# Attention and mixer on one core: score couples of neighbouring pairs of heads, grouped two by two

## Chip, cores, metric

One core of a Trainium2 chip. The metric is the device time of one execution in microseconds (us). A kernel's quoted time is the median of its runs, and the runs of "before" beside it were made on the same chip. PE is the engine of the matmuls, DVE the vector engine, ACT the scalar engine, POOL the GpSimd engine; L363 is line 363 of the kernel.

## The reference

Cosine attention over 8 batches, 12 heads, 448 positions, 64 dimensions a head, followed by a mixer (a low-rank product along the sequence, then a two-layer perceptron with residual):

```python
q_n = q / (norm(q) + 1e-6);  k_n = k / (norm(k) + 1e-6)
scores = q_n @ k_n.T / tau
attn = softmax(scores)                    # exp(s - max) / (sum + 1e-9)
x = (attn @ v) laid out as [batch, seq, 768]
h = x.transpose(0, 2, 1) @ U @ V          # rank 32, along the sequence
u = x + h.transpose(0, 2, 1)
out = u + relu(u @ w_ch1) @ w_ch2         # 768 -> 3072 -> 768
```

## The kernel before

Two heads form a pair; there are 48 pairs, 6 a batch. For one pair, 64 + 64 dimensions lie on 128 partitions. Key chunks 0, 1 and 2 are scored by a *couple*: two matmuls of 64 contraction rows, one head on partitions 0 to 63 and one on 64 to 127, which run side by side (their starts lie 3 to 4 ns apart in the traces, and a couple behind a couple starts 0.196 us after it). The last 64 keys of both heads are packed into one matmul of 128 rows (chunk 3).

```python
def step_S(b, p, cs):                                   # scores and exponentials
    t = qkT[(b, p)];  e = E[(b * NP + p) % 2]
    for c in cs:
        sc = psum.tile([128, 2, 512], FP, name="sc", tag="ps_sc", bufs=2)
        if c == 3:                                      # full rows (L274)
            nc.tensor.matmul(out=sc[:, 0, 0:S], lhsT=t[:, 1, 384:512], rhs=t[:, 0, 0:S], ...)
            nc.scalar.activation(out=e[:, 6, 0:S], in_=sc[:, 0, 0:S], func=AF.Exp)
            continue
        for h in range(2):                              # a couple, half rows (L282)
            r = slice(64 * h, 64 * h + 64)
            nc.tensor.matmul(out=sc[:, h, 0:S], lhsT=t[r, 1, c * 128:(c + 1) * 128],
                             rhs=t[r, 0, 0:S], start=True, stop=True)
        nc.scalar.activation(out=e[:, 2 * c:2 * c + 2, 0:S], in_=sc[:, :, 0:S], func=AF.Exp)
```

The other steps of a pair, all with full-row matmuls: T (transposes of q and k, copied out by DVE as qkT), V in two halves V0 and V1 (probabilities by values, L302 and L309; DVE then makes X from the result), A (low-rank product with U, L331, and X moved into `up`, L342), H (product with V, L347). The mixer of the batch before (`mp`, L363 with w1 and L390 with w2) is cut into parts of six matmuls, which a list `fill` hands out between the steps by weights:

```python
for n in range(NPAIR + 1):
    ...
    parts = [now and S(0, 1), prev and V0, now and S(2, 3), prev and V1,
             nxt and T(n + 1), prev and A, prev and H]           # abridged
    weights = (2, 2, 2, 2, 2, 2, 1)
    for i, (fn, w) in enumerate(zip(parts, weights)):
        fn()
        # hooks for norms and loads at place i of pair n: after.pop((n, i)) ...
        # then as many mixer parts from `fill` as the weights give
```

In batch 0 (pairs 0 to 5) and at pair 6 there is no mixer work yet, so PE has nothing to fill its waits with.

Of the kernel before, what the change touches and what calls it, by code (L numbers as in the profile page):

```python
# [22 lines left out]
def kernel(  # L23
# [22 lines left out]
    NP = H // 2  # L46
# [207 lines left out]
    def step_T(b, p):  # L254
        gi, j = group_of[(b, p)]
        qn, kb, _ = norm[gi]
        tp = psum.tile([128, 8, 128], BF, name="tp", tag="ps_x", bufs=1)
        for i, t in ((0, qn), (1, kb)):
            for c in range(4):
                nc.tensor.transpose(out=tp[:, 4 * i + c, :], in_=t[:, j, c, :, :], identity=ident)  # L260
        t = work.tile([128, 2, 512], BF, name="qkT", tag="qkT", bufs=3)
        nc.vector.tensor_copy(out=t.rearrange("p a b -> p (a b)"),  # L262
                              in_=tp.rearrange("p a b -> p (a b)"))
        qkT[(b, p)] = t
        est.pe(0.46)
        est.dve(0.69)

    def step_S(b, p, cs):
        t = qkT[(b, p)]
        e = E[(b * NP + p) % 2]  # L270
        for c in cs:
            sc = psum.tile([128, 2, 512], FP, name="sc", tag="ps_sc", bufs=2)
            if c == 3:
                nc.tensor.matmul(out=sc[:, 0, 0:S], lhsT=t[:, 1, 384:512], rhs=t[:, 0, 0:S],  # L274
                                 start=True, stop=True)
                nc.scalar.activation(out=e[:, 6, 0:S], in_=sc[:, 0, 0:S], func=AF.Exp)
                est.pe(0.3)
                est.act(0.56)
                continue
            for h in range(2):  # L280
# [4 lines that stand above are left out]
            est.pe(0.25)  # L285
            est.act(0.93)
# [3 lines left out]
    def step_V(b, p, half):  # L290
        gi, j = group_of[(b, p)]
        vv = norm[gi][2]
        e = E[(b * NP + p) % 2]
        if half == 0:
            X_of[(b, p)] = work.tile([128, 4, 128], BF, name="X", tag="X", bufs=2)
        X = X_of[(b, p)]
        bank = psum.tile([128, 512], FP, name="av", tag="ps_av", bufs=1)
        av_of[(b, p)] = bank
        av = bank[:, 0:4 * (D + 1)].rearrange("p (i h d) -> p i h d", i=2, h=2)
        for i in range(2):  # L300
            ic = 2 * half + i
            nc.tensor.matmul(out=av[:, i, :, :], lhsT=e[:, 6, ic * 128:(ic + 1) * 128],  # L302
                             rhs=vv[:, 2 * j:2 * j + 2, 3, :],
                             start=(i == 0), stop=False, skip_group_check=True)
        for i in range(2):
            ic = 2 * half + i
            for h in range(2):
                for c in range(3):
                    nc.tensor.matmul(out=av[:, i, h, :],  # L309
                                     lhsT=e[:, 2 * c + h, ic * 128:(ic + 1) * 128],  # L310
                                     rhs=vv[:, 2 * j + h, c, :],
                                     start=False, stop=(i == 1 and h == 1 and c == 2),
                                     skip_group_check=True)
        rd = work.tile([128, 4, 1], FP, name="rd", tag="rd", bufs=4)
        nc.vector.reciprocal(out=rd, in_=av.rearrange("p i h d -> p (i h) d")[:, :, D:D + 1])  # L315
        nc.vector.tensor_mul(  # L316
            X[:, 2 * half:2 * half + 2, :].rearrange("p i (h d) -> p i h d", h=2),
            av[:, :, :, 0:D],
            rd.rearrange("p (i h) o -> p i h o", h=2).to_broadcast([128, 2, 2, D]))
        est.pe(0.52)  # L320
        est.dve(0.6)


    def u_of(b):
        return uE if b % 2 == 0 else uO

    def step_A(b, p):
        X = X_of[(b, p)]
        ap = av_of[(b, p)][:, 384:512]
        for c in range(4):  # L330
            nc.tensor.matmul(out=ap, lhsT=U_sb[:, c, :], rhs=X[:, c, :],  # L331
                             start=False, stop=(c == 3), skip_group_check=True)
        A = work.tile([128, 128], BF, name="A_sb", tag="A_sb", bufs=2)
        nc.scalar.copy(out=A, in_=ap)  # L334
        A_of[(b, p)] = A
        est.pe(0.44)
        est.act(0.3)
        up = psum.tile([128, S], FP, name="up", tag="ps_x", bufs=1)
        up_of[(b, p)] = up
        for c in range(4):  # L340
            n = 128 if c < 3 else 64
            nc.tensor.matmul(out=up[:, c * 128:c * 128 + n], lhsT=X[:, c, :], rhs=ident[:, 0:n],  # L342
                             start=(c == 0), stop=False, skip_group_check=True)

    def step_H(b, p):
        up = up_of[(b, p)]
        nc.tensor.matmul(out=up, lhsT=A_of[(b, p)], rhs=V_sb,  # L347
                         start=False, stop=True, skip_group_check=True)
        nc.vector.tensor_copy(out=u_of(b)[:, p, 0:S], in_=up)  # L349
        est.pe(0.19)  # L350
        est.dve(0.62)
        if b % 2 == 1 and p == NP - 1:
            nc.vector.tensor_copy(out=uO[:, :, S:512], in_=uE[:, :, 384:S])


    def steps_m1(b):
        u = u_of(b)
        o = 64 if b % 2 == 0 else 0

        def one(f):  # L360
            mp = psum.tile([128, S], FP, name="mp", tag="ps_m", bufs=2)
            for cc in range(CC):
                nc.tensor.matmul(out=mp, lhsT=w1_sb[:, cc, f * 128:(f + 1) * 128],  # L363
                                 rhs=u[:, cc, 0:S], start=(cc == 0), stop=(cc == CC - 1))
            est.pe(1.13)
            if est.act_first(0.55, 0.62):
                nc.scalar.activation(out=relu[:, f, o:o + S], in_=mp, func=AF.Relu)  # L367
            else:
                nc.vector.tensor_scalar_max(out=relu[:, f, o:o + S], in0=mp, scalar1=0.0)  # L369

        return [lambda f=f: one(f) for f in range(NC)]
# [59 lines left out]
    pairs = [(b, p) for b in range(B) for p in range(NP)]  # L431
# [50 lines left out]
    for gi in range(1, len(groups)):  # L482
        m, n, g = first_pair[gi], groups[gi][2], preps[gi]
# [23 lines left out]
    for n in range(NPAIR + 1):  # L507
        b, p = pairs[n] if n < NPAIR else (B, 0)
        prev = pairs[n - 1] if n > 0 else None
        now, nxt = n < NPAIR, n + 1 < NPAIR  # L510
        parts = [
            now and (lambda: step_S(b, p, (0, 1))),
            prev and (lambda: step_V(*prev, 0)),
            now and (lambda: step_S(b, p, (2, 3))),
            prev and (lambda: step_V(*prev, 1)),
            nxt and (lambda: step_T(*pairs[n + 1])),
            prev and (lambda: step_A(*prev)),
            prev and (lambda: step_H(*prev)),
        ]
        weights = [w if part else 0 for part, w in zip(parts, (2, 2, 2, 2, 2, 2, 1))]  # L520
        left = NP - p + 0.85 if p else 0.85
        nf = len(fill) if p == 0 else int(round(len(fill) / left))
        given = acc = 0
        for fn in after.pop((n, -1), []):
            fn()
        for i, (fn, w) in enumerate(zip(parts, weights)):
            if fn:
                fn()
            for g in after.pop((n, i), []):
                g()  # L530
            acc += w
            want = nf * acc // sum(weights)
            for _ in range(min(want - given, len(fill))):
                fill.pop(0)()
            given = want
        if p == 0 and n > 0:
            while fill:
                fill.pop(0)()
            fill.extend(steps_m1(b - 1) + steps_m2(b - 1))
# [38 lines left out]
```

## Time and profile before

| | before |
|---|---|
| median of 6 runs (3 of them made beside the changed kernel) | 648.82 us (648.52 to 649.09) |
| span of the profiled run | 646.9 us |
| PE busy | 94% of the span |
| DVE, ACT busy | 42%, 42% |
| mean granted clock of PE | 0.995 |

### The profile page before, as it was taken

Reading aid. Unit: us, or ns where it says so; the run is one execution under the profiler, and the core shown is the slowest. Engines: PE = TensorE matmul, PEld = TensorE weight load, DVE = VectorE, ACT = ScalarE, POOL = GpSimd, SP = SyncE. Lnnn points to the kernel's source line nnn. Section 1 sums busy time; section 2 is a strip of 40 time slices with the busy share of each in tenths; the row PEclk is TensorE's granted clock in tenths of the full one; section 3 lists DMA queues with packets and bytes.
Section 4 is the critical chain, followed back from the end, with each engine's and each line's share of the span. In section 5 each row is a group of like instructions: output and inputs, shape, how many; then the busy total and the mean of one; then the engine's idle time right before and its main releaser. Section 6 shows DMA issues by size and latency. Waiting matters only on the chain.

```text
span 646.9 us, 12173 instructions
## 1 busy us (share of the span) xinstructions
PE 609.4 (94%) x5160; PEld 360.4 (56%) x5160; DVE 273.3 (42%) x524; ACT 273.3 (42%) x501; POOL 195.2 (30%) x158
## 2 busy tenths in 40 slices
PE   1467999999999999999999999999999999999997
PEld 0244556655566556665566655665566555665564
DVE  4788335355244455364353453463442543210000
ACT  2465554345433454345433455334523454324310
POOL 7877244043141341340431431431404401000000
PEclk9997999999999999999999999999999999999999
DMA  7899991350315420161315302044311100001011
GB/s 195 196 220 234 233 241 43 98 147 4 83 35 126 110 73 16 32 168 48 86 26 135 95 24 79 25 117 105 87 25 26 50 1 1 25 25 26 1 50 49
DMA packets 51782, 54.33 MB, mean 84 GB/s; under 512 B 5552, under 2 KB 48112, under 8 KB 51728
## 3 DMA queue, kind: packets, MB, share of 16 engines
q1 hardware_dynamic: 44288, 43.14, 26.1%
q0 software_dynamic: 7120, 10.18, 8.6%
q8 instruction: 40, 0.66, 0.4%
q10 hardware_dynamic: 320, 0.23, 0.1%
q14 instruction: 14, 0.11, 0.1%
HBM read 52.02 MB, written 11.01 MB: 97 GB/s over the span
## 4 chain that ended last, share of the span: by engine, by line
PE 91%; DVE 6%; DMA 1%; ACT 0%; issue 0%; SPq 0%; ACTq 0%
PE mp L390 34%; PE mp L363 34%; PE av L309 5%; PE sc L282 5%; PE tp L260 3%; PE sc L274 2%; DVE qn L241 2%; PE av L302 2%; PE av L331 2%; DVE ss L215 1%; PE up L342 1%; PE mp L399 1%; PE up L347 1%; DVE qkT L262 1%; DVE X L316 1%; DMA kst<-in_k_dram 1%
## 5 line engine op out<-in xcount | busy, mean ns | idle before, releaser
L390 PE MATMUL mp<-w_sb,relu 128*128 128x384 bf16 x1344 | 246.8, 326 | 0.0
L390 PEld LDWEIGHTS <-relu 128*128 128x128 bf16 x1344 | 123.7, 98 | 77.9 <-issue 7.4
L241 POOL TENSOR_TENSOR kb<-kst,inv 128x512 bf16<-128x512 f32 x46 | 59.3, 1310 | 336.3 <-DVE inv L233 284.8
L363 PEld LDWEIGHTS <-w_sb 128*128 128x128 bf16 x1152 | 106.0, 98 | 92.9 <-issue 7.8
L284 ACT ACTIVATE E<-sc 128x896 bf16<-128x896 f32 x144 | 126.3, 917 | 46.3 <-PE sc L282 46.2
L367 ACT ACTIVATE relu<-mp 128x448 bf16<-128x448 f32 x156 | 84.7, 543 | 134.4 <-PE mp L363 134.4
L363 PE MATMUL mp<-uE,w_sb 128*128 128x448 bf16 x576 | 122.9, 353 | 1.1 <-DVE uE L349 1.1
L363 PE MATMUL mp<-uO,w_sb 128*128 128x448 bf16 x576 | 118.0, 353 | 0.0
L404 ACT COPY o_sb<-mp 128x384 f32<-128x384 f32 x50 | 23.9, 478 | 109.0 <-PE mp L399 109.0
L215 DVE TENSOR_REDUCE ss<-sq 128x16 f32<-128x1024 f32 (+1 forms) x50 | 58.1, 1166 | 3.3 <-ACT sq L207 3.3
L315 DVE RECIPROCAL rd<-av 128x4 f32<-128x4 f32 x96 | 17.1, 178 | 95.4 <-PE av L309 95.4
L241 DVE TENSOR_TENSOR qn<-qst,inv 128x512 bf16<-128x512 f32 x48 | 53.4, 1150 | 0.0
L282 PE MATMUL sc<-qkT 64*128 64x448 bf16 x288 | 45.5, 368 | 8.2 <-DVE qkT L262 6.1
L210 POOL TENSOR_TENSOR sq<-kst 128x1024 f32<-128x1024 f32 x23 | 52.0, 2262 | 2.7 <-DMA qst<-in_q_dram 2.7
L309 PE MATMUL av<-v,E 128*128 128x65 bf16 x1152 | 52.8, 195 | 0.0
L369 DVE TENSOR_SCALAR relu<-mp 128x448 bf16<-128x448 f32 x36 | 22.5, 625 | 67.0 <-PE mp L363 67.0
L262 DVE COPY qkT<-tp 128x1024 bf16<-128x1024 bf16 x48 | 33.0, 687 | 36.7 <-PE tp L260 36.7
L309 PEld LDWEIGHTS <-E 128*128 128x128 bf16 x1152 | 46.2, 98 | 0.0
L210 POOL TENSOR_TENSOR sq<-qst 128x1024 f32<-128x1024 f32 x23 | 43.5, 1892 | 0.0
L316 DVE TENSOR_TENSOR X<-av,rd 128x256 bf16<-128x256 f32 x96 | 40.8, 425 | 3.3
L334 ACT CAST A_sb<-av 128x128 bf16<-128x128 f32 x48 | 12.6, 263 | 61.7 <-PE av L331 61.7
L349 DVE CAST uO<-up 128x448 bf16<-128x448 f32 x24 | 14.9, 623 | 53.9 <-PE up L347 53.9
(66 smaller groups left out, 394.7 us busy)
## 6 DMA issues: line engine op xcount, KB each, us to landing
out_dram<-o_sb SPq DMA_DIRECT2D x54, 192.0 KB, 2.7
w_sb<-in_moe_w_ch_dram POOLq DMA_DIRECT2D x8, 1152.0 KB, 27.0
qst<-in_q_dram SPq DMA_DIRECT2D x23, 256.0 KB, 3.9
vst<-in_v_dram SPq DMA_DIRECT2D x46, 128.0 KB, 2.9
kst<-in_k_dram SPq DMA_DIRECT2D x44, 128.0 KB, 3.7
qst<-in_q_dram SPq DMA_DIRECT2D x23, 192.0 KB, 4.0
vst<-in_v_dram SPq DMA_DIRECT2D x46, 96.0 KB, 2.8
kst<-in_k_dram SPq DMA_DIRECT2D x44, 96.0 KB, 3.4
```

What stands on the lines that cost most here:

```text
L210: nc.gpsimd.tensor_mul(sq[:, 0:self.nh * 4, :], self.flat(t), self.flat(t))
L215: nc.vector.reduce_sum(self.ss[:, j, 0:self.nh * 4], self.sq[j][:, 0:self.nh * 4, :], axis=AX.X)
L241: eng.tensor_mul(o[:, j, :, :, :], t[:, 2 * j:2 * j + 2, :, :].rearrange("p h c d -> p c h d"), iv.unsqueeze(3).to_broadcast([128, 4, 2, D]))
L262: nc.vector.tensor_copy(out=t.rearrange("p a b -> p (a b)"), in_=tp.rearrange("p a b -> p (a b)"))
L282: nc.tensor.matmul(out=sc[:, h, 0:S], lhsT=t[r, 1, c * 128:(c + 1) * 128], rhs=t[r, 0, 0:S], start=True, stop=True)
L284: nc.scalar.activation(out=e[:, 2 * c:2 * c + 2, 0:S], in_=sc[:, :, 0:S], func=AF.Exp)
L309: nc.tensor.matmul(out=av[:, i, h, :], lhsT=e[:, 2 * c + h, ic * 128:(ic + 1) * 128], rhs=vv[:, 2 * j + h, c, :], start=False, stop=(i == ...
L316: nc.vector.tensor_mul(X[:, 2 * half:2 * half + 2, :].rearrange("p i (h d) -> p i h d", h=2), av[:, :, :, 0:D], rd.rearrange("p (i h) o -> ...
L363: nc.tensor.matmul(out=mp, lhsT=w1_sb[:, cc, f * 128:(f + 1) * 128], rhs=u[:, cc, 0:S], start=(cc == 0), stop=(cc == CC - 1))
L367: nc.scalar.activation(out=relu[:, f, o:o + S], in_=mp, func=AF.Relu)
L390: nc.tensor.matmul(out=mp, lhsT=relu[:, f, r0:r0 + 128], rhs=w2_sb[:, f, half * HC:(half + 1) * HC], start=(f == 0), stop=False, skip_grou ...
L404: nc.scalar.copy(out=o[:, cols], in_=mp)
```

## The change

The intent: run score couples of two neighbouring pairs back to back, so that PE changes between half rows and full rows less often. From pair 6 on, two pairs have three groups of two couples, in place of two groups of two and two single couples.

```diff
-        parts = [
-            now and (lambda: step_S(b, p, (0, 1))),
...
-        weights = [w if part else 0 for part, w in zip(parts, (2, 2, 2, 2, 2, 2, 1))]
+        if n < NP:
+            order = [ ... as before ... ]
+        elif n % 2 == 0:
+            order = [
+                (0, 2, now and (lambda: step_S(b, p, (0, 1)))),
+                (1, 2, lambda: step_V(*prev, 0)),
+                (2, 2, now and (lambda: step_S(b, p, (3,)))),
+                (4, 2, nxt and (lambda: step_T(*pairs[n + 1]))),
+                (3, 2, lambda: step_V(*prev, 1)),
+                (5, 1, lambda: step_A(*prev)),
+                (-2, 1, nxt and (lambda: (step_S(b, p, (2,)), step_S(*pairs[n + 1], (0,))))),
+                (6, 1, lambda: step_H(*prev)),
+            ]
+        else:
+            order = [
+                (0, 2, lambda: step_S(b, p, (1, 2))),
+                (1, 2, lambda: step_V(*prev, 0)),
+                (2, 2, lambda: step_S(b, p, (3,))),
+                ... V1, T, A, H as before ...
+            ]
+        parts = [fn for _, _, fn in order]
+        weights = [w if fn else 0 for _, w, fn in order]
```

Note that in even pairs the transposes T also move ahead of V1, and that V1 comes closer to A.

More of the change, by code (lines that the diff above doesn't have):

```diff
@@ L510 @@
         now, nxt = n < NPAIR, n + 1 < NPAIR
-        parts = [
-            now and (lambda: step_S(b, p, (0, 1))),
-            prev and (lambda: step_V(*prev, 0)),
-            now and (lambda: step_S(b, p, (2, 3))),
-            prev and (lambda: step_V(*prev, 1)),
-            nxt and (lambda: step_T(*pairs[n + 1])),
-            prev and (lambda: step_A(*prev)),
-            prev and (lambda: step_H(*prev)),
-        ]
-        weights = [w if part else 0 for part, w in zip(parts, (2, 2, 2, 2, 2, 2, 1))]
+        if n < NP:
+            order = [
+                (0, 2, now and (lambda: step_S(b, p, (0, 1)))),
+                (1, 2, prev and (lambda: step_V(*prev, 0))),
+                (2, 2, now and (lambda: step_S(b, p, (2, 3)))),
+                (3, 2, prev and (lambda: step_V(*prev, 1))),
+                (4, 2, nxt and (lambda: step_T(*pairs[n + 1]))),
+                (5, 2, prev and (lambda: step_A(*prev))),
+                (6, 1, prev and (lambda: step_H(*prev))),
+            ]
+        elif n % 2 == 0:
+            order = [
+                (0, 2, now and (lambda: step_S(b, p, (0, 1)))),
+                (1, 2, lambda: step_V(*prev, 0)),
+                (2, 2, now and (lambda: step_S(b, p, (3,)))),
+                (4, 2, nxt and (lambda: step_T(*pairs[n + 1]))),
+                (3, 2, lambda: step_V(*prev, 1)),
[4 more added lines that the diff above has]
+        else:
+            order = [
+                (0, 2, lambda: step_S(b, p, (1, 2))),
+                (1, 2, lambda: step_V(*prev, 0)),
+                (2, 2, lambda: step_S(b, p, (3,))),
+                (3, 2, lambda: step_V(*prev, 1)),
+                (4, 2, nxt and (lambda: step_T(*pairs[n + 1]))),
+                (5, 2, lambda: step_A(*prev)),
+                (6, 1, lambda: step_H(*prev)),
+            ]
+        parts = [fn for _, _, fn in order]
+        weights = [w if fn else 0 for _, w, fn in order]
         left = NP - p + 0.85 if p else 0.85
```

## The prediction

> **What bounds the kernel now.** I read the page first, then the PE's list of waits, then the chain of work in order of time around a score step. The page's busy lines, its slice line of PE and its chain line:
>
> ```profile
> PE 609.4 (94%) x5160; PEld 360.4 (56%) x5160; DVE 273.3 (42%) x524; ACT 273.3 (42%) x501; POOL 195.2 (30%) x158
> ...
> PE   1467999999999999999999999999999999999997
> ...
> PE 91%; DVE 6%; DMA 1%; ACT 0%; issue 0%; SPq 0%; ACTq 0%
> ```
>
> PE is full from the fifth slice of 16 us on, and the end is set by PE. The list of PE's waits names 32.9 us in all; the same list asked for 66 us onwards is empty. So after batch 0 there is no wait to take away: only PE's own time counts, and it is read from spacings of matmuls, because neighbours overlap in their recorded durations (353 ns recorded against a spacing of 0.19 us below). Two stretches of the chain, a lone score couple followed by the full-row score matmul, and two couples back to back (columns: start us, us, what):
>
> ```profile
> 301.96 0.38 PE mp L363 x2
> 302.34 0.29 PE sc L282 x2
> 302.63 0.30 PE sc L274
> 302.93 1.14 PE mp L363 x6
> ```
> ```profile
> 311.29 1.13 PE mp L363 x6
> 312.42 0.49 PE sc L282 x4
> 312.91 1.24 PE mp L363 x6
> ```
>
> A mixer matmul of 448 columns takes its turn every 0.189 us (1.13/6). A couple, two 64-row matmuls side by side, should cost one such turn, since its two matmuls start 3 to 4 ns apart. It costs 0.29, and the full-row matmul that follows costs 0.30, not 0.19. With two couples together the four cost 0.49 = 2 x 0.19 + 0.11, and the six full-row matmuls after them 1.24 instead of 1.13. So each passage from full rows to half rows costs about 0.10 us, each passage back about 0.11, and the step from couple to couple nothing.
>
> [...] in the first listing 0.29 + 0.30 - 2 x 0.189 = 0.21 us for in and out, in the second 0.49 + 1.24 - 2 x 0.189 - 1.13 = 0.22. [...]
>
> **The change, part by part.** Arithmetic and operands stay; from pair 6 on the order differs, and the order of both programs shows the same 5160 matmuls.
>
> [...] A pair has three couples (0, 1, 2) and one full-row score matmul (3). Before, each pair runs {0,1} and later {2} then 3: two groups. After, an even pair runs {0,1}, then 3 alone, and near its end {2 with 0 of the next pair}; the odd pair runs {1,2}, then 3. Three groups in two pairs instead of four. Counting runs of couples in the built order gives 95 before and 74 after, 21 fewer: even pairs 6 to 46. Each is worth one passage in and out: 21 x 0.214 = 4.5 us. That is on the path wherever PE never waits, so the whole of it from pair 8 on.
>
> Moved, first: the exponentials. At 20 of the 21 sites (pair 6 apart), between the joined group {2,0'} and {1',2'} lie two mixer parts and the matmul with V. From couple 0' to couple 1' that is 0.28 (way out) + the parts + 0.10 (way in): with two w2 parts 12 x 0.163 + 0.189 + 0.37 = 2.5 us, with two w1 parts 12 x 0.189 + 0.189 + 0.37 = 2.8. Couple 2' comes 0.20 later, and it needs the buffer that the exponential of 0' frees. In this trace the exponential starts 0.40 to 0.54 us after its couple (0.54 where a relu is before it in ACT's queue), a second in a row starts 0.81 later (the two in a row of pair 27 take 1.72 together), so that of 0' ends 0.4 to 0.54 - 0.2 + 0.81 + 0.92 = 1.9 to 2.1 us after couple 0'. In batch 0 a waiting matmul starts about 0.05 us after such an end (exponential ending at 39.49, matmul at 39.54). Needed at 2.7, there at 2.1: slack 0.6. No wait.
>
> Moved, second: step V1 now comes after the transposes and just one or two mixer parts ahead of the low-rank step A, which needs V1's result from DVE. In the trace V1's last matmul is followed by the reciprocal after 0.23 us (0.28 beside w1 parts) and the product X is complete 0.87 us (0.91) after that matmul starts; A starts 0.055 after X. That makes 0.93 (0.97). Distance now: at six sites one w2 part, 0.03 + 0.98 = 1.01; at three sites one w1 part, 1.17; elsewhere two parts, 2 or more. Before, the shortest was 2.4 (but for the last two pairs). So 0.08 us of slack at six sites, if DVE is free when V1 ends. What stands before V1 in DVE's queue is the copy of the transposes, 0.69, and the inversion of norms, 0.18 + 0.35, together 1.2 from 0.2 after the transposes; V1 ends 1.5 after them. Free by 0.1 to 0.25. Charge: 0 us, with up to 0.3 at each if I am wrong.
>
> Moved, third: the seam at pair 6, where there are no mixer parts to fill in. Here I walk all queues with the durations of this trace. The lines of DVE there now:
>
> ```profile
> 58.32 1.21 DVE L215 TENSOR_REDUCE ss<-sq 128x16 f32<-128x1024 f32 x1
> 59.56 0.18 DVE L218 TENSOR_SCALAR ss<-ss 128x32 f32<-128x32 f32 x1
> ...
> 60.52 0.35 DVE L233 RECIPROCAL inv<-ss 128x32 f32<-128x32 f32 x1
> 60.79 0.63 DVE L262 COPY qkT<-tp 128x1024 bf16<-128x1024 bf16 x1
> 61.33 2.69 DVE L241 TENSOR_TENSOR qn<-qst,inv 128x512 bf16<-128x512 f32 x2
> ```
>
> After: the copy of the transposes goes at 59.66, the inversion 60.3 to 60.87, V1's reciprocal only then, X done at 61.42, A at 61.47 (60.34 now), its second half straight after instead of at 61.47, the joined group at 61.97, V's product at 62.45. Then couples 1' and 2' directly: they wait for exponentials that end near 63.3 and 64.1, and mixer work begins at 64.44 (62.43 now). But now its sixth matmul waits 1.06 us for DVE's copy of u and goes at 64.61; after, that copy is done in time and the sixth goes at 65.4. Net 0.79 later with one couple more done (0.19): a loss of 0.6 us, once.
>
> Added: nothing. ACT and DVE get the same work; a few evacuations change engine (103 rows of relu and output copies on ACT in the built order before, 112 after, where repeats share a row), and neither engine bounds.
>
> Sum: -4.5 + 0.6 = -3.9. 648.8 - 3.9 = 644.9 us, 0.6% less.
>
> **The rivals.** (1) [...] grouped couples use both score buffers at once, so {1',2'} could stand on PE for 0'. For it: that is what happens in batch 0, and pair 6 will. Against: 0.6 us of slack with filler in between, and PE's empty list of waits after 66 us. If my slack were all wrong by a microsecond, 20 sites x 0.4 = 8 us, and the time would be 653. (2) A waits for X: nine tight sites. Against: DVE is 42% busy and each slack came out positive. For: 0.08 us is thin. At 0.3 us each 2.7 us are lost, 647.6. (3) [...] the full-row matmul 3, now alone, might keep its 0.30. Against: that 0.30 is the way back from half rows, seen in front of mixer matmuls as well. If it did, nothing is gained: 649.4. (4) Pair 6 goes better than walked: 644.3.
>
> **Range and chances.** The saving is arithmetic on spacings that repeat to a few ns, so the range comes from the seam (0 to 1.2) and from thin slacks (0 to 2): 643.8 to 646.6. Faster by over 2% would need 13 us, three times all that 21 passages hold: 0.01. Slower by over 2% needs a stall of 0.8 us at every site: 0.02. Within 2%: 0.97.
>
> **What would show it.** In the profile after: four half-row matmuls in every group from pair 6 on; 0.49 for each and 0.19 for a lone full-row score; a list of waits from 66 us on that is still empty, or has only hundredths for A on X. The seam: PE waits near 62.5 to 64.2 for exponentials, and the wait for u gone. The span up to the first mixer work longer, all later stretches shorter by 0.2 us in every two pairs. Wrong, if PE shows many waits of score matmuls on ACT after 66 us, or if lone couples and joined ones prove equally dear.

The sum is -4.5 + 0.6 = -3.9 us, estimated from spacings and durations in the trace of the kernel before. The prediction reads PE from starts and spacings, and walks the other engines in the program's order, which was the assumption; at the seam it put A at 61.47 us, 61.9 with the 0.4 by which the run came later to it, and A came at 62.0.

## More of the kernel before

PE's granted clock is the share of full speed at which it was allowed to run.

The page's row of PE's granted clock, in tenths per slice of 16 us, is short; it will matter:

```profile
PEclk9997999999999999999999999999999999999999
```

A digit below 9 in the fourth slice says that PE ran with less than its full clock for part of the time from 48 to 65 us.

## The result, and the profile after

The changed kernel took 646.32 us, the median of 6 runs (645.90 to 647.66). The ratio to the kernel before is 0.9964, with a 95% interval of 0.9951 to 0.9977. Ratios here are the mean time of one kernel's fast runs over that of the other's in the same rounds, so not quite the ratio of the medians. The gain is 2.5 us by the medians, against 3.9 predicted; it is clear of noise, and well within the 2% that the prediction gave.

The chain of work of the changed kernel in order of time (start us, us, what) has a lone full-row score matmul, and a joined group with the next group two mixer parts behind it:

```profile
302.57 1.14 PE mp L363 x6
303.71 0.19 PE sc L274
303.89 2.27 PE mp L363 x12
```
```profile
310.93 0.48 PE sc L282 x4
311.42 1.24 PE mp L363 x6
312.66 0.19 PE up L347
312.85 1.14 PE mp L363 x6
313.98 0.48 PE sc L282 x4
314.47 1.24 PE mp L363 x6
```

The full-row score matmul now costs its bare turn of 0.19, and the mixer after it costs 2.27 for 12, nothing extra. Each group costs 0.48 and leaves 0.10 in the matmuls after it (1.24 in place of 1.14). The group that comes close behind starts without a wait.

To see where the time went I cut both traces at the first 65-column V matmul of chosen pairs (us, from the matmuls' starts; "seam" is the stretch in which the new order begins):

| stretch | before | after | difference |
|---|---|---|---|
| start to the first transpose | 13.06 | 13.30 | +0.24 |
| first transpose to V0 of pair 5 (batch 0) | 43.77 | 43.93 | +0.16 |
| V0 of pair 5 to that of pair 7 (seam) | 20.39 | 23.30 | **+2.91** |
| pair 7 to pair 45 (38 pairs) | 474.93 | 470.86 | **-4.07** |
| pair 45 to pair 47 | 21.69 | 21.47 | -0.22 |
| pair 47 to the end | 73.01 | 73.02 | +0.01 |

The steady part gained exactly what was predicted: 4.07 us over 38 pairs is 0.214 for every two. The seam gave most of it back in this run. (The traced run of the changed kernel was the slowest of its six, 647.66 us, so that the rows add up to -1.0 us, and not to the 2.5 of the medians.) The list of PE's waits of the changed kernel (us in total, times, longest) has one new large entry, the 2.3:

```profile
PE av L331 <- DVE X L316: 4.4, 4, 2.3
```

The timeline of PE at the seam of the changed kernel shows where it lies (start us, us; in brackets the idle time before and its releaser):

```profile
59.20 0.54 PE L309 MATMUL av<-v,E 128*128 128x65 bf16 x12
62.03 0.38 PE L331 MATMUL av<-X,U_sb 128*128 128x128 bf16 x4 [2.29 <-DVE X L316]
62.25 0.36 PE L342 MATMUL up<-ident,X 128*128 128x128 bf16 x4
62.54 0.66 PE L282 MATMUL sc<-qkT 64*128 64x448 bf16 x4
63.13 0.55 PE L347 MATMUL up<-V_sb,A_sb 128*128 128x448 bf16 x1
63.92 0.56 PE L282 MATMUL sc<-qkT 64*128 64x448 bf16 x2 [0.23 <-ACT E L284]
64.72 0.56 PE L282 MATMUL sc<-qkT 64*128 64x448 bf16 x2 [0.25 <-ACT E L284]
65.21 2.42 PE L363 MATMUL mp<-uE,w_sb 128*128 128x448 bf16 x6
```

The 2.29 us wait of A and the two short waits of couples for ACT were in the walk. What was not is the last line: six mixer matmuls take 2.42 us of recorded time here, where 1.30 is usual. The window view gives the clock (columns: stretch, us, busy time and count of PE, its weight loads, DVE, ACT, POOL, then the granted clock):

```profile
56.10:62.80 6.70, 3.87 (x58) 2.61 (x57) 5.95 (x12) 2.90 (x7) 3.30 (x4) 1.00 1.15 235
62.90:69.60 6.70, 6.22 (x33) 2.76 (x30) 2.87 (x5) 3.89 (x5) 6.32 (x4) 0.50 1.15 233
```

In the 6.7 us after the wait PE had half its clock, just as the mixer work began. In the kernel before, the only half-clock window on record (the traces have the clock from about 30 us on) lay from 49.6 to 56.5, in batch 0, and the same stretch ran at full clock:

```profile
63.00:70.00 7.00, 5.94 (x57) 3.37 (x56) 2.77 (x6) 3.91 (x8) 5.60 (x4) 1.00 1.15 230
```

The clock row of the page has, accordingly, a second dent (the 8 in the fifth slice):

```profile
PEclk9997899999999999999999999999999999999999
```

### The profile page after: what moved, and what is told of

Its sections match the earlier page's. It is cut to its first block, busy times and chain, and to the rows that moved or that the text cites. A ratio compares the mean times of both kernels' runs of the same rounds, so it can differ in the third digit from the quotient of the medians.

```text
span 645.9 us, 12169 instructions
## 1 busy us (share of the span) xinstructions
PE 608.9 (94%) x5160; PEld 364.2 (56%) x5160; DVE 267.2 (41%) x512; ACT 282.3 (44%) x513; POOL 194.7 (30%) x158
## 4 chain that ended last, share of the span: by engine, by line
PE 92%; DVE 5%; DMA 1%; ACT 1%; SPq 0%; issue 0%
PE mp L363 34%; PE mp L390 34%; PE av L309 5%; PE sc L282 5%; PE tp L260 3%; PE av L302 2%; PE av L331 2%; PE up L342 2%; DVE ss L215 1%; PE mp L399 1%; PE up L347 1%; PE sc L274 1%; DVE qn L241 1%; DVE qkT L262 1%; DMA qst<-in_q_dram 1%; DVE X L316 1%
## 5 line engine op out<-in xcount | busy, mean ns | idle before, releaser
L367 ACT ACTIVATE relu<-mp 128x448 bf16<-128x448 f32 x162 | 88.2, 544 | 132.9 <-PE mp L363 132.9
L284 ACT ACTIVATE E<-sc 128x896 bf16<-128x896 f32 x144 | 124.1, 917 | 20.4 <-PE sc L282 20.0
L363 PE MATMUL mp<-uE,w_sb 128*128 128x448 bf16 x576 | 124.6, 356 | 0.0
L404 ACT COPY o_sb<-mp 128x384 f32<-128x384 f32 x56 | 26.7, 477 | 99.7 <-PE mp L399 99.7
L282 PE MATMUL sc<-qkT 64*128 64x448 bf16 x288 | 42.6, 370 | 8.5 <-DVE qkT L262 6.1
L369 DVE TENSOR_SCALAR relu<-mp 128x448 bf16<-128x448 f32 x30 | 18.7, 625 | 41.4 <-PE mp L363 41.4
```

Source lines behind the costliest of these rows:

```text
L363: nc.tensor.matmul(out=mp, lhsT=w1_sb[:, cc, f * 128:(f + 1) * 128], rhs=u[:, cc, 0:S], start=(cc == 0), stop=(cc == CC - 1))
L367: nc.scalar.activation(out=relu[:, f, o:o + S], in_=mp, func=AF.Relu)
L404: nc.scalar.copy(out=o[:, cols], in_=mp)
```

## The experiments

All gave correct results except the two "narrow" ones, which are wrong.

### 1. The changed kernel again

No edit.

> The changed kernel once more, as it is. My theory: in the steady part it gains 0.21 us per two pairs as predicted, and at the seam at pair 6 it loses more than I predicted, because step A waits 2.3 us there and PE's granted clock then falls to half for one or two windows of 3.4 us. As these windows do not fall alike in every run, this kernel's times should spread by over 1 us (645.9 to 647.7 before), low where the mean granted clock is 0.994 and high where it is 0.989, and the median should be near 646.3. Rival: the spread is noise of the chip; then the kernel before should spread as much in the same rounds, and the time should not go with the clock.

Measured: 647.23 us (646.43 to 647.71, 5 runs), ratio 0.9974 (0.9962 to 0.9987), before 648.61 (648.31 to 649.28) in 9 runs. The profiled run again had a half-clock window from 62.4 to 69.3, and by the same cuts as above its seam was 23.30 and pair 7 to 45 was 470.86, both as in the first trace of this kernel to the hundredth. (Such windows are 6.8 us long in both traces of this kernel, and 3.4 in those of experiments 2 and 3.) The spread was 1.3 us, against 1.0 in the kernel before. The expectation that time goes with the mean clock failed: of two runs with a mean clock of 0.995 one took 647.10 and one 647.43, as slow as those with 0.989. The kernel before spread nearly as much in the same rounds, which is what the rival, noise of the chip, expected. The mean says how long the half clock lasted, not on which work it fell, and only one run in each set has a trace that shows that; so what spreads the times stays open.

### 2. The new order from pair 8

```diff
-        if n < NP:
+        if n < NP + 2:
```

> The new order starts at pair 8 in place of pair 6; pairs 6 and 7 keep the old order. It saves 20 passages in place of 21. My theory (the seam costs what is missing): 648.8 - 20 x 0.214 = 644.5 us, spread like that of the kernel before (0.3 us), one half-clock window only, wait of A on X in pair 6 back at 0.7 us. Rival (the seam is harmless, each passage is worth less than 0.21 us or something in the steady part loses it): 646.3 + 0.1, no better than the changed kernel.

Measured: 644.85 us (644.03 to 645.37), ratio 0.9938 (0.9925 to 0.9950). It beats the changed kernel by 2.4 us on the same chip, with one passage less saved. Pair 7 to 45 is again 470.86. Its seam took 20.97, and even that has a half-clock window of 3.4 us in it (62.1 to 65.6), a second one; so "one window only" was not met in this run, and the spread of 1.3 us was larger than expected. The rival, that the seam is harmless, is out.

### 3. The reordering alone, without joined groups

```diff
-                (0, 2, lambda: step_S(b, p, (1, 2))),        # odd pairs
-                (2, 2, lambda: step_S(b, p, (3,))),
+                (0, 2, lambda: step_S(b, p, (0, 1))),
+                (2, 2, lambda: step_S(b, p, (2, 3))),
# even pairs: (3,) becomes (2, 3); the joined group is taken out; T stays ahead of V1
```

> The old grouping of couples ({0,1}, then {2} with 3) in all pairs, but in even pairs from 6 on the transposes come before V1 as in the changed kernel. My theory: moving V1 gains nothing in the steady part and loses at the seam, where A waits some 2 us for X: 649 to 651 us, steady stretches equal to those of the kernel before within 0.1 us per two pairs. Rival (the reordering itself gives the gain, not the joined groups): about 646.

Measured: 649.10 us (648.95 to 650.76), ratio 1.0006 (0.9993 to 1.0020). Pair 7 to 45 took 474.93, the figure of the kernel before to the hundredth: moving T and V1 gives and costs nothing in the steady part. Its seam took 21.48, 1.1 more than before, with a wait of A on X of 1.9. So the gain is from the joined groups alone, and a loss at the seam comes with the reordering (this trace, too, had a half-clock window there, from 63.4 to 66.8).

### 4. PE kept busy through the wait at the seam

```diff
-                (3, 2, lambda: step_V(*prev, 1)),
+                (3, 2, lambda: (step_V(*prev, 1), keep_busy(10) if n == NP else None)),
# keep_busy: 10 matmuls of 448 columns with ident and U_sb into a free mp buffer, never read
```

> The changed kernel with 10 useless matmuls of 448 columns (1.9 us of PE work) after V1 of pair 6, where PE waits 2.3 us for X anyway; their result is never read. My theory (the wait lets the granted clock fall to half, and that is what the seam costs beyond the 0.6 us): no half-clock window near 63 us, mean clock 0.994 to 0.995, and 644.9 us, the figure that the prediction gave, 1.4 less than the changed kernel, with small spread. Rival (the lost time is the wait of A itself and of the couples behind it): no faster than the changed kernel, 646.3 or more.

Measured: 645.04 us (644.11 to 645.77), ratio 0.9942 (0.9930 to 0.9955), 2.2 less than the changed kernel in the same rounds although 10 matmuls were added. The timeline of PE at its seam:

```profile
57.99 0.54 PE L309 MATMUL av<-v,E 128*128 128x65 bf16 x12
58.37 2.05 PE L511 MATMUL mp<-U_sb,ident 128*128 128x448 bf16 x10
60.82 0.38 PE L331 MATMUL av<-X,U_sb 128*128 128x128 bf16 x4 [0.40 <-DVE X L316]
...
63.81 1.31 PE L363 MATMUL mp<-uE,w_sb 128*128 128x448 bf16 x6
```

A starts 2.83 us after the V1 matmuls here (60.82 - 57.99), and 2.83 in the changed kernel (62.03 - 59.20): the added work neither hurried nor held up A, which waits for DVE. But the six mixer matmuls take 1.31, not 2.42, and the clock is full:

```profile
63.00:70.00 7.00, 6.56 (x66) 4.00 (x64) 2.17 (x6) 4.41 (x8) 5.01 (x3) 1.00 1.15 231
```

By the cuts, the seam took 20.97 in place of 23.30. So 2.3 us of the seam's loss were the half clock, and 0.6 remain (20.97 - 20.39). The old order's seam itself measures 20.36 to 20.61 in the traces of experiments 6 to 8, so these tenths are uncertain by some 0.2: against the first trace of experiment 7 (20.61), which like this one has no half clock in batch 0 or the seam, 0.4 remain. With the passage that is saved there added, that is 0.6 to 0.8, where the prediction had 0.6. Only one of the five runs has a trace; that the others were mostly spared too is read from their median. In this traced run there was no half-clock window on record before the end, so batch 0 was 0.7 shorter too; the same happened by chance in other runs (experiment 7), so that I do not put down to the edit.

### 5. More passages in place of fewer

```diff
-            now and (lambda: step_S(b, p, (0, 1))),
+            now and (lambda: (step_S(b, p, (0,)), fill and fill.pop(0)(), step_S(b, p, (1,)))),
```

> The kernel before with a mixer part put between couples 0 and 1 of every pair from 7 on: three groups a pair in place of two, 41 passages more (136 runs of couples in the built order, 95 before), nothing else. This takes the disputed cost up in place of down. My theory (each passage into and out of half rows costs 0.214 us whatever surrounds it): 648.6 + 41 x 0.214 = 657.4 us, and no wait of PE after 66 us. Rival (the gain of the change came from something else than the number of passages): within 1 us of 648.6.

Measured: 659.76 us (659.21 to 660.75, 4 runs), ratio 1.0172 (1.0157 to 1.0188), so 10.9 more than before in place of 8.8. The chain shows a lone couple costing the same as ever, whichever full-row work follows:

```profile
305.29 0.29 PE sc L282 x2
305.59 1.24 PE mp L363 x6
306.83 0.30 PE sc L282 x2
```

The rest is a side effect, which the list of waits after 66 us has: taking mixer parts out of turn left pairs 12, 24 and 36 with no work between T and A.

```profile
PE up L342 <- DVE qkT L262: 1.7, 3, 0.6
```

From the starts, `up` is delayed by 2.16 us in all, and 41 x 0.21 + 2.2 = 10.8. The cost of a passage holds in both directions; the expectation of no wait did not.

### 6. The joined group later

From pair 8, with the joined group after H instead of before:

```diff
-                (-2, 1, nxt and (lambda: (step_S(b, p, (2,)), step_S(*pairs[n + 1], (0,))))),
                 (6, 1, lambda: step_H(*prev)),
+                (-2, 1, nxt and (lambda: (step_S(b, p, (2,)), step_S(*pairs[n + 1], (0,))))),
```

> The new order from pair 8 on, but in even pairs the joined group stands after the product with V instead of before it, so that one mixer part in place of two parts and that product lies ahead of the couples {1',2'}. Passages as in the run from pair 8. My walk of ACT's queue says: couple 2' comes 0.28 + 0.98 (or 1.14) + 0.10 + 0.20 = 1.56 to 1.72 us after couple 0', and the exponential of 0' ends 1.9 to 2.1 after it, so PE waits 0.25 to 0.55 us for ACT at each of 20 sites: 5 to 11 us in the list of waits after 66 us, and 650 to 656 us. Rival (ACT has far more room than I walked): 644.9 as from pair 8, no such wait.

Measured: 656.91 us (656.58 to 657.14, 4 runs), ratio 1.0123 (1.0109 to 1.0137), just above the range expected. With the same joined groups, one mixer part and the product H less ahead of the second group turn the gain into a loss. The waits after 66 us:

```profile
PE up L347 <- ACT A_sb L334: 3.1, 14, 0.4
PE sc L282 <- ACT E L284: 2.4, 10, 0.3
```

They add up to 5.5 us, but pair 7 to 45 is 11.7 longer than in experiment 2. Read from starts, the second couple of the delayed group comes 0.44 to 0.61 us after the first, where 0.196 is usual: 6.6 us over 20 sites, inside the 5 to 11 expected. The product H, which I had overlooked, now follows A too closely, and waits for ACT's copy of A: 5.5 us by the starts. Together 12.0. The list of waits shows less than half of that, because it counts idle time only from a matmul's recorded end, and that lies 0.16 us behind its turn (353 ns recorded, 189 ns a turn). The rule for PE: look for lost time in the spacing of starts, not only in the list of waits.

### 7. Joined groups from pair 8, with V1 ahead of T as before

```diff
-                (4, 2, nxt and (lambda: step_T(*pairs[n + 1]))),
                 (3, 2, lambda: step_V(*prev, 1)),
+                (4, 2, nxt and (lambda: step_T(*pairs[n + 1]))),
```

> The new order from pair 8 on, but V1 ahead of the transposes as before; couples joined all the same. My theory: the gain is from joining alone; the copy of the transposes (0.2 + 0.69 us after them, then DVE free) is done before the joined group comes 1.4 us or more after the transposes, so 644.9 as from pair 8 and no wait after 66 us. Rival (the earlier transposes are needed, because couple 0' would wait for its copy of the transposed queries and keys): a wait of score on that copy at many of 20 sites, 0.2 us or more each, 649 or more.

> The fastest version once more on another occasion: 644.0 to 645.4 us by the spread that the run from pair 8 showed, which is the same program up to pair 8; 4.0 to 4.8 under the kernel before. If it stays at 644.0 to 644.3 the narrow spread was no luck.

Measured: 644.19 us (644.00 to 644.27, 5 runs), ratio 0.9927 (0.9914 to 0.9939), and on the second occasion 644.74 (644.11 to 644.83, 5 runs), ratio 0.9938 (0.9924 to 0.9952), before 648.45. Pair 7 to 45 took 470.88 both times, with no wait after 66 us. So the transposes need not move, and this version does the same as experiment 2 with the smallest edit. The narrow spread of the first occasion was partly luck. It beats both kernels; with what certainty it beats experiment 2 stays open, since the two differ in no steady stretch by more than 0.02 us.

### 8. Experiment 2 with PE kept busy in batch 0

```diff
-    nxt and (lambda: step_T(*pairs[n + 1]))
+    nxt and (lambda: (step_T(*pairs[n + 1]), keep_busy(3) if 2 <= n <= NP else None))
# in step_A, ahead of the `up` matmuls of pairs 1 to 5: keep_busy(3)
```

> The new order from pair 8 on, with three useless matmuls in each of the two waits of PE in batch 0 and at pair 6 (30 in all, 5.7 us of PE work, where PE waits for X and for the copy of the transposes). My theory: the run from pair 8 still had half-clock windows near 42 and 62 us; with PE kept busy these go, mean clock 0.997 or more, and the mixer's first matmuls run at full clock: 643.5 to 644.3 us, the fastest of all. Rival (the windows cost nothing there, or the useless matmuls hold up those that wait): 644.9 or more.

Measured: 644.61 us (643.67 to 645.07), ratio 0.9932 (0.9919 to 0.9944). The half clock went: the mean clock was 0.999 to 1.0 in all five runs. The time did not get under that of experiments 2 and 7, so this expectation failed. In the trace, batch 0 (V0 of pair 0 to pair 5) took 29.72, as with a half-clock window (29.71 before), against 28.98 in experiment 7's trace without one: so the useless matmuls seem to cost there what the clock gave; no run separates the two. And the spread of 1.4 us stayed with the clock practically always full, so the clock is not the only thing that differs between runs. In the traces of all these kernels the first transpose comes between 12.86 and 13.99 us after the start, before any instruction that the edits touch; that is a second source.

### 9. What a passage consists of

As experiment 7, with fewer columns of keys in the half-row matmuls from pair 8 on (wrong results, one run each: 645.74 us with 96 columns, 645.11 with 64):

```diff
-                nc.tensor.matmul(out=sc[:, h, 0:S], lhsT=t[r, 1, c * 128:(c + 1) * 128],
+                nc.tensor.matmul(out=sc[0:w, h, 0:S], lhsT=t[r, 1, c * 128:c * 128 + w],
# w = 96 or 64 from pair 8 on; the exponential is cut to w partitions too
```

> What a passage consists of. As join_no_swap, but from pair 8 on each half-row score matmul has 96 columns of keys in place of 128 (a quarter of the scores of those three key chunks is missing: the result is wrong on purpose[...]). A passage in costs 0.096 us over a turn, and the recorded load of the couple's weights takes 0.092 to 0.093. Theory L: [...] if the recorded load gets shorter or longer with 96 columns, the passage in changes by the same number of ns (24 ns shorter if the load goes with the columns). Theory D: [...] the passage in stays at 96 ns whatever the load takes.

> The same with 64 columns of keys[...]. Theory L: passage in down by half of the load (some 46 ns) if the load is halved; the passage out, where a load of full rows follows, unchanged at 0.103. Theory D: both unchanged.

The traces print these half-row matmuls as `64*128`, `64*96` and `64*64`, so more than the count of columns may differ between the three kernels. The weight load got longer, not shorter, with fewer columns. In the groups of weight loads (line, engine, operation, shapes, count, busy us, mean ns), first experiment 7, then 96 columns, then 64:

```profile
L282 PEld LDWEIGHTS <-qkT 64*128 64x128 bf16 x288 | 9.2, 95 | 24.9 <-issue 15.1 <-DVE qkT L262 6.7
```
```profile
L283 PEld LDWEIGHTS <-qkT 64*96 64x96 bf16 x240 | 9.8, 118 | 13.4 <-issue 10.6
```
```profile
L283 PEld LDWEIGHTS <-qkT 64*64 64x64 bf16 x240 | 8.3, 104 | 13.4 <-issue 10.6
```

The first load of a group takes 92 to 93 ns, 116 and 103. From the start of the last full-row matmul ahead of a group (of 448 columns, 20 groups) to that of the second couple it is 485 ns, 509 and 496 on the mean: longer by 25 and 11, where the load is longer by 23 and 10. From the second couple to the next full-row matmul, the way out, it stays at 285 in all three. Over the 38 pairs the stretch grew by 1.42 and 0.65 us, 25 and 11 ns for each of 57 groups. The first couple's own start moved by -3 ns only, so by the letter of the expectation theory D would have won. But this start is recorded 4 ns after that of the couple's own weight load and cannot show how long the load takes; the delay shows in the couple behind, which starts 111, 112 and 112 ns after the first load ends. (Its own load, which also got longer, ended 90, 64 and 77 ns before it, so it did not wait for that.) What the runs show is that the way in goes with the first weight load, to within 2 ns, which speaks for theory L. That a fixed part stands beside it they do not exclude, and for the way out (285 - 189 = 96 ns, about a full-row load of 98) there is no test. The traces do show one thing in common: between mixer matmuls the next weight load starts 2 ns after the matmul before it, a whole turn ahead; into a group, behind a matmul of 448 columns, it starts 281 ns after it, and out of a group 281 ns after the second couple, in all three kernels.

## Why the prediction was right or wrong

- *PE bounds, and its own time counts.* Right. After the seam no wait is found, either in the list or in the spacings.
- *A passage costs 0.214 us, 21 of them go.* Right: 0.214 for every two pairs measured, taken away (-4.29 us over 20 times two), and 41 put in (experiment 5). What this time consists of the prediction could not show; experiment 9 shows that at least the way in goes with a weight load (with first loads of 116 and 103 ns in place of 93 it grew by 25 and 11 ns).
- *ACT has 0.6 us of room for the exponentials.* Right in kind and near in size: one mixer part less made the second couple wait 0.25 to 0.42 (experiment 6), where a part and H, 1.2 to 1.3 us, had gone from between: 0.7 to 1.1 of room.
- *A's slack on X, thin at nine sites.* Right: in the changed kernel A follows the mixer part at 162 to 163 ns (w2) or 189 to 190 (w1), its bare turn, at every site.
- *The seam costs 0.6 us once.* This is the term of the sum that was mis-sized. The net seam, with the passage saved there taken off, was to be 0.6 - 0.2 = +0.4 us, and it measured +2.9. The queues went as walked: shifted by the 0.4 us by which this run came later to V0 of pair 5, A was predicted at 61.9 and came at 62.0, mixer work at 64.8 and came at 65.2. The durations did not hold: all were taken at full clock, but after 6.7 us in which PE was 58% busy (3.87 of 6.70), with a pause of 2.29, the clock fell to a half. Experiment 4 takes the half clock away and leaves +0.4 to +0.6 net, near the walk. The slice row of the clock before had shown that the clock falls in this phase, and the prediction did not use it.
- *The range.* The low end of 643.8 to 646.6 had no room for an effect of the clock, the high end happened to have it, so the median fell inside. That was luck: single runs lay above it (647.66), and so did the median of the second set of five (647.23). Nor is the range the sum of its own terms: 0 to 1.2 for the seam and 0 to 2 for the slacks would have given 644.3 to 647.5.

## What to carry to other kernels

On a kernel that PE bounds, count the passages between half-row and full-row matmuls and join those of one kind, also across independent pieces of work; here each passage in and out together cost a little more than a matmul of 448 columns (0.214 us against 0.189). Start such a reordering only where there is work to fill the gaps (here the seam, which has none, took 2.9 us more), and leave enough of it behind each joined group for the exponentials to empty the buffers: with one part and one matmul less there, waits for exponentials alone cost 6.6 us, more than the whole gain of 4. When a reordering opens a pause on PE, look at the granted clock of the microseconds after it, not only at the pause: here it was 0.50 for 6.8 us after a pause of 2.29. None of the half-clock windows quoted above, of 3.4 and 6.8 us, had a pause of PE over 2.3 us in the 10 us ahead of it, and that of the kernel before had none over 1.02.
